# Where the first down product of a pair of chunks stands on TensorE

## The chip, the core and the metric

The kernel runs on one core of a Trainium2 chip. Its time is the device time of one execution in microseconds. Three runs of the kernel before the change took 606.92, 608.14 and 609.78 us; the median, 608.14 us, is the time before.

## What is computed

The input is `x` with 2048 tokens of 512 channels, in float32. Two branches read it and a gate mixes them:

```python
g = _sigmoid((x * gate_w).sum(-1, keepdims=True))
a = _A_ref(x, A_wqkv, A_wo)     # attention, 32 heads of 16, over 8 positions 2 apart
b = (_gelu(x @ w_gate) * (x @ w_up)) @ w_down      # 512 -> 1792 -> 512
return g * a + (1 - g) * b
```

The second branch, the FFN, is where the change lies. Its hidden layer has 1792 columns, which the kernel cuts into 14 chunks of 128.

## The kernel before

**Tokens.** The 2048 tokens are worked on in two halves of 1024, called `par` 0 and `par` 1. A half has two blocks `b` of four tiles `t` of 128 tokens. `ffn(0)` is the first FFN and `ffn(1)` the second; between them stand the projections of the second half's queries, keys and values (line 189). The attention itself runs on VectorE beside all of this.

**Precision.** A float32 operand is split into a high and a low part, and a product is three matmuls of 128x128 by 128x512: high times high, high times low, low times high. For a chunk's down weights the high part is made by ScalarE (line 484). The low part is a negated copy by ScalarE (line 481), to which a transfer issued by POOL adds the raw weights (line 482, `d<-r`). The gate and up weights `g` are made in the same way (lines 452, 453 and 457); two such transfers, of 384 and 512 KB, belong to a chunk, and one of 256 KB to its down weights.

**One chunk.** `gate_up` does the gate and up products of a chunk in seven block products of a 2x2 scheme, each of six matmuls (line 495): `a11`, `s1`, `s2`, `a12`, `s4`, `s3` and `a22`. The last of them, `a22`, is put off: `late` holds it and `fourth()` emits it in the next chunk, between that chunk's `s1` and `s2`. Between the products ScalarE applies the activation, VectorE adds and multiplies, and `hidden` leaves the chunk's hidden values as a high part `hh` (line 511) and a low part `hl` (line 512), one pair for each block `b`.

**The down product.** Chunks are taken in pairs; `gr` numbers the pairs from 0 to 6. While chunk `f` is done, `down(par, f // 2 - 1, t, b)` multiplies the pair before it with its down weights: chunk 6, for instance, begins the downs of pair 2, which are chunks 4 and 5. One call is six matmuls (line 538), three for each chunk of the pair (`i` is 0 or 1): `hh` with the high weights, `hh` with the low ones, `hl` with the high ones. For `b` 0 they add into one of four PSUM banks, `acc0` to `acc3`, which stay open through all seven pairs; for `b` 1 they go to a bank `p`, which ScalarE fills from `rt` and empties to it (lines 532 and 554). The first call of a pair, with `b` and `t` 0, is emitted in an even chunk right behind that chunk's `a11` product. The seventh pair's calls stand behind the loop over the chunks, after the last `fourth()`.

**What sets the order.** The order on each engine isn't that of the program text. A scheduler (the tile framework, with a model of the engines' times) takes the emitted instructions and may put a matmul ahead of others that were emitted before it, as soon as it holds its operands for ready. `ordered(ins, other)` forbids that for one pair of instructions: `ins` must then stand behind `other` on their engine. It adds no semaphore. `paced(ins)` adds one: the instruction then waits until the last emitted matmul is done. `LAST` holds the last matmul that was emitted. Work of the attention is pulled in by `pull` at a low priority.

In `down`, lines 538 to 542 are the ones of interest. `LAST` is set after every matmul, so a call for which the condition holds is chained as a whole: its first matmul stands behind the last one emitted before it, and its six follow in the order of the text. The condition takes `gr` 1, with `b` and `t` 0, in the first FFN. The other transfers that the prediction speaks of are `keep_parts` (line 470, `ws<-g`) and the loads of raw weights (lines 423 to 428).

Of the kernel before, what the change touches and what calls it, by code (L numbers as in the profile page):

```python
# [47 lines left out]
def tile_gated_mix(ctx: ExitStack, tc: tile.TileContext, xt, wqkv, wff, wo, out):  # L48
# [11 lines left out]
    def tl(tag, dt=F32):  # L60
        return pool.tile([P, COLS.get(tag, 512)], dt, name=tag, bufs=BUFS[tag])
# [5 lines left out]
    def bank(tag):  # L67
        return psum.tile([P, 512], F32, name=tag, bufs=BUFS.get(tag, 1))
# [291 lines left out]
    def ordered(ins, other):  # L360
        after(ins, other, mybir.DependencyClass.NoSync)
# [39 lines left out]
    def pull(budget, key=None):  # L401
        credit[0] += budget
        while credit[0] > 0 and (key is None or key not in done):
            with tc.high_priority(offset=-BEHIND):
                c = next(fill, None)
            if c is None:
                credit[0] = 0.0
                return
            credit[0] -= c
        if key:  # L410
            credit[0] = 0.0
# [105 lines left out]
    def pace(par, f):  # L517
        return PACE[2 if par else f > 5]
# [8 lines left out]
    def down(par, gr, t, b):  # L527
        if b == t == gr == 0:
            ACC.update((t, bank(f"acc{t}")) for t in range(BT))
        pp = bank("p") if b else ACC[t]  # L530
        if b and gr:
            nc.scalar.activation(pp, RT[BT + t], AF.Copy)  # L532
        ts = slice(t * P, (t + 1) * P)
        for i in range(2):
            hh_, hl_ = Hs[2 * gr + i, b]
            d = WD[2 * gr + i]
            for n, (a, w) in enumerate(((hh_, d[:, :512]), (hh_, d[:, 512:1024]), (hl_, d[:, :512]))):
                ins = nc.tensor.matmul(pp, a[:, ts], w, start=(i == 0 and n == 0 and gr == 0),  # L538
                                       stop=(i == 1 and n == 2), skip_group_check=True)
                if gr == 1 and b == t == 0 and not par:  # L540
                    ordered(ins, LAST[-1])
                LAST[:] = [ins]
        jj = BT * b + t
        if gr == NG - 1 and par:
            nc.scalar.activation(pp, pp, AF.Copy, scale=gc[:, par, jj:jj + 1])
            ACC[jj] = pp
        elif gr == NG - 1:
            st = tl("s")
            nc.scalar.activation(st, pp, AF.Copy, scale=gc[:, par, jj:jj + 1])
            nc.gpsimd.dma_start(out_v[2 * jj], st)  # L550
        elif b:
            if gr == 0:
                RT[BT + t] = tl("rt")
            nc.scalar.activation(RT[BT + t], pp, AF.Copy)  # L554
        pull(1.2 * pace(par, 2 * gr + 2))
# [87 lines left out]
    def ffn(par):  # L643
# [3 lines left out]
        for f in range(FC):  # L647
# [5 lines left out]
            if f > 1:  # L653
                pieces = [[lambda b=b, i=i: down(par, f // 2 - 1, f % 2 * 2 + i, b)] for b in range(2) for i in range(2)]
            else:
                tile_ = (lambda jj: project_one(1, jj)) if par else values
                pieces = [[lambda jj=jj: tile_(jj) for jj in jjs]
                          for jjs in (((0, 1), (2, 3), (4, 5), ()),
                                      ((6,), (7,), (), ()) if par else ((6, 7), (), (), ()))[f]]
# [48 lines left out]
        for b in range(2):  # L708
            for t in range(BT):
                down(par, NG - 1, t, b)  # L710
                if par and t == 0:
                    oT[0, b] = channels(par, 0, b)
                if not par and not b:
                    split_kq() if t % 2 else again(0, 1 + t)
                elif not par and b:
                    again(1, (2, 3, 0, 1)[t])
# [454 lines left out]
```

## Time and profile before

| | us |
|---|---|
| median of three runs | 608.14 |
| lowest and highest run | 606.92, 609.78 |
| the profiled execution, its own time | 609.76 |
| its span, from the first to the last instruction | 608.0 |
| TensorE busy with matmuls | 598.2 |
| VectorE busy | 526.5 |
| ScalarE busy | 382.9 |
| POOL busy | 79.1 |

The profiled execution took 609.76 us, and its span is 608.0 us of them. In a timeline row stand the start, the time, the engine, the line, the operation with its tiles, and how many instructions were merged; the bracket behind it tells the engine's idle time before and who ended it. Matmuls are pipelined: one of 512 columns is shown with 0.39 us, but the next starts 0.227 us after it.

### The profile page before, as it was taken

How to read it: one execution, taken by the hardware profiler on the slowest of the kernel's cores; microseconds unless marked ns; L12 is line 12 of the kernel's file. 1: busy time of each engine (PE TensorE's matmuls, PEld its weight loads, DVE VectorE, ACT ScalarE, POOL GpSimd, SP SyncE). 2: the span in 40 equal slices, each digit the busy share in tenths (PEclk: the TensorE clock that was granted, in tenths of full speed). 3: DMA queues.
4: the chain of work that ended last, by engine and by line, in shares of the span. 5: the costliest groups of instructions: out<-in, count | busy, mean ns of one | idle time of the engine just before them, and what ended most of it. 6: DMA issues, size and time to landing. Idle time of an engine off the chain costs nothing.

```text
span 608.0 us, 8192 instructions
## 1 busy us (share of the span) xinstructions
PE 598.2 (98%) x2802; PEld 498.2 (82%) x2802; DVE 526.5 (87%) x611; ACT 382.9 (63%) x650; POOL 79.1 (13%) x106
## 2 busy tenths in 40 slices
PE   9999999999999999989999999999999999999997
PEld 6889977788888887877899888888888888888885
DVE  5997969999898998798989988789899999999941
ACT  5845557777679776857364356566866676677531
POOL 0501001111111111102000001111101111101200
PEclk9999999999999999999999999999999999999999
DMA  7289896989889888976789979686888768937823
GB/s 279 85 252 246 241 275 172 271 237 271 206 248 260 223 255 230 253 205 181 253 218 335 252 221 271 146 256 158 228 207 213 207 182 217 259 88 207 125 50 138
DMA packets 84741, 131.03 MB, mean 216 GB/s; under 512 B 8030, under 2 KB 52317, under 8 KB 84700
## 3 DMA queue, kind: packets, MB, share of 16 engines
q1 hardware_dynamic: 63310, 94.01, 47.7%
q0 software_dynamic: 12096, 31.40, 27.3%
q10 hardware_dynamic: 9294, 5.11, 2.8%
q8 instruction: 22, 0.36, 0.2%
q14 instruction: 19, 0.16, 0.1%
HBM read 67.18 MB, written 36.77 MB: 171 GB/s over the span
## 4 chain that ended last, share of the span: by engine, by line
PE 71%; DMA 12%; issue 8%; DVE 4%; ACT 3%; SPq 1%; ACTq 0%; POOL 0%; POOLq 0%; DVEq 0%
PE p L495 29%; PE p L538 9%; PE acc L189 9%; PE acc L538 9%; PE p L767 5%; DMA d<-r 4%; DMA g<-raw 3%; PE p L834 3%; PE acc L834 3%; DMA ws<-g 3%; DVE prod L290 2%; PE p L189 2%; PE acc L767 2%; DMA kq<-qs 1%; DMA vs<-hl 1%
## 5 line engine op out<-in xcount | busy, mean ns | idle before, releaser
L495 PE MATMUL p<-S,g 128*128 128x512 f32 x672 | 166.5, 390 | 0.0
L495 PEld LDWEIGHTS p<-S,g 128*128 128x128 f32 x672 | 125.7, 188 | 26.5 <-ACT rt L554 0.5
L495 PE MATMUL p<-A,g 128*128 128x512 f32 x504 | 127.6, 390 | 0.1
L495 PEld LDWEIGHTS p<-A,g 128*128 128x128 f32 x504 | 94.3, 188 | 20.4 <-DMA g<-raw 0.6
L290 DVE TENSOR_TENSOR prod<-kq 128x2048 f32<-128x2048 f32 x32 | 73.0, 2281 | 12.3 <-DMA kq<-qs 4.6
L453 POOL DMA_DIRECT2D g<-raw x40 | 34.8, 870 | 319.0 <-ACT g L452 180.5
L331 DVE TENSOR_TENSOR prod<-v,lg 128x2048 f32<-128x2048 f32 x32 | 72.9, 2277 | 1.8 <-PE acc L538 1.3
L293 DVE TENSOR_REDUCE lg<-prod 128x128 f32<-128x2048 f32 x32 | 73.0, 2282 | 0.3
L538 PE MATMUL p<-d,hh 128*128 128x512 f32 x224 | 68.0, 390 | 1.0 <-ACT p L532 0.5
L538 PE MATMUL acc<-d,hh 128*128 128x512 f32 x224 | 61.3, 392 | 3.3 <-DMA d<-r 2.9
L538 PEld LDWEIGHTS acc<-d,hh 128*128 128x128 f32 x224 | 41.8, 188 | 13.5 <-DMA d<-r 3.8
L538 PEld LDWEIGHTS p<-d,hh 128*128 128x128 f32 x224 | 41.9, 188 | 10.5 <-ACT p L532 0.9
L457 ACT ACTIVATE g<-raw 128x1024 fp32r<-128x1024 f32 (+1 forms) x40 | 39.5, 990 | 13.3 <-PE p L495 13.3
L509 DVE TENSOR_TENSOR c<-c 128x512 f32<-128x512 f32 x56 | 38.2, 683 | 9.2 <-ACT c L606 8.8
L505 DVE TENSOR_TENSOR c<-p,s 128x512 f32<-128x512 f32 x56 | 37.9, 682 | 8.1 <-PE p L495 8.1
L500 ACT ACTIVATE s<-p 128x512 f32<-128x512 f32 x56 | 33.2, 592 | 18.1 <-PE p L495 16.5
L452 ACT ACTIVATE g<-raw 128x1024 fp32r<-128x1024 f32 (+1 forms) x40 | 39.5, 986 | 7.9 <-DVE raw L434 6.9
L538 PE MATMUL p<-d,hl 128*128 128x512 f32 x112 | 42.3, 390 | 0.0
L512 DVE TENSOR_TENSOR hl<-c,hh 128x512 fp32r<-128x512 f32 x56 | 38.3, 685 | 4.5 <-ACT hh L511 4.2
L511 ACT ACTIVATE hh<-c 128x512 fp32r<-128x512 f32 x56 | 35.1, 626 | 7.4 <-DVE c L509 6.5
L554 ACT ACTIVATE rt<-p 128x512 f32<-128x512 f32 x48 | 28.1, 592 | 18.1 <-PE p L538 17.8
L335 DVE TENSOR_TENSOR prod<-prod 128x1024 f32<-128x1024 f32 x32 | 39.0, 1219 | 0.3
(193 smaller groups left out, 916.2 us busy)
## 6 DMA issues: line engine op xcount, KB each, us to landing
g<-raw POOLq DMA_DIRECT2D x27, 512.0 KB, 6.1
raw<-wff SPq DMA_DIRECT2D x42, 256.0 KB, 3.4
ws<-g SPq DMA_DIRECT2D x14, 768.0 KB, 5.6
g<-ws SPq DMA_DIRECT2D x14, 768.0 KB, 5.1
r<-wff SPq DMA_DIRECT2D x28, 256.0 KB, 3.7
d<-r POOLq DMA_DIRECT2D x26, 256.0 KB, 7.2
g<-raw POOLq DMA_DIRECT2D x13, 384.0 KB, 7.5
v<-vs SPq DMA_DIRECT2D x8, 512.0 KB, 7.3
```

The costliest lines, as they stand in the source:

```text
L189: LAST[:] = [nc.tensor.matmul(ps[:, :cn], a[:, t], w[:, c0:c0 + cn], start=(kc == 0 and n == 0), stop=(kc == KC - 1 and n == 2))]
L290: paced(nc.vector.tensor_tensor(prod, spans(k, jj), q[:, jj:jj + 2, None, :].to_broadcast([P, 2, W, UC]), op=OP.mult))
L293: nc.vector.tensor_reduce(two_of(lg, jj), prod.rearrange("p j w (h d) -> p (j w) h d", d=DH), axis=AX.X, op=OP.add)
L331: paced(nc.vector.tensor_tensor(prod.rearrange("p j w (h d) -> p (j w) h d", d=DH), spans(v, jj).rearrange("p j w (h d) -> p j w h d", d=D ...
L335: nc.vector.tensor_tensor(prod[:, :, :4], prod[:, :, :4], prod[:, :, 4:], op=OP.add)
L452: nc.scalar.activation(lo, raw, AF.Copy, scale=-1.0)
L457: ins = nc.scalar.activation(hi, raw, AF.Copy)
L495: LAST[:] = [nc.tensor.matmul(ps, w_, a_, start=(start and kc == 0 and n == 0), stop=(kc == 1 and n == 2), skip_group_check=True)]
L509: nc.vector.tensor_tensor(ge, ge, up, op=OP.mult)
L512: nc.vector.tensor_tensor(hl_, ge, hh_.bitcast(F32), op=OP.subtract)
L538: ins = nc.tensor.matmul(pp, a[:, ts], w, start=(i == 0 and n == 0 and gr == 0), stop=(i == 1 and n == 2), skip_group_check=True)
L767: ins = nc.tensor.matmul(pa, a, b, start=(first and n == 0), stop=(last and n == 2), skip_group_check=True)
```

## The change

The condition for the chain loses its bound to the second pair. It then holds for `gr` 1 to 6 in the first FFN, so for five more calls: those of pairs 2 to 5, behind `a11` of chunks 6, 8, 10 and 12, and that of pair 6, behind `a22` of chunk 13. The second FFN (`par` 1) isn't touched.

```diff
             for n, (a, w) in enumerate(((hh_, d[:, :512]), (hh_, d[:, 512:1024]), (hl_, d[:, :512]))):
                 ins = nc.tensor.matmul(pp, a[:, ts], w, start=(i == 0 and n == 0 and gr == 0),
                                        stop=(i == 1 and n == 2), skip_group_check=True)
-                if gr == 1 and b == t == 0 and not par:
+                if gr and b == t == 0 and not par:
                     ordered(ins, LAST[-1])
                 LAST[:] = [ins]
```

## Prediction, made before the changed kernel was run

> **What bounds the kernel now.** I read the page's busy times first, then the stretches of the span, then what TensorE (PE) waited for.
>
> ```profile
> PE 598.2 (98%) x2802; PEld 498.2 (82%) x2802; DVE 526.5 (87%) x611; ACT 382.9 (63%) x650; POOL 79.1 (13%) x106
> 45.00:105.00 60.00, 59.20 (x350) 51.92 (x349) 51.60 (x52) 36.37 (x72) 5.78 (x7) 1.00 0.83 236
> 105.00:285.00 180.00, 176.40 (x771) 143.85 (x770) 163.11 (x200) 133.35 (x211) 28.67 (x35) 1.00 0.87 236
> 285.00:370.00 85.00, 85.00 (x466) 74.35 (x465) 76.91 (x90) 41.62 (x81) 7.10 (x10) 1.00 0.85 253
> 370.00:550.00 180.00, 180.00 (x796) 149.14 (x795) 163.86 (x172) 117.30 (x191) 20.93 (x25) 1.00 0.76 203
> ```
>
> The rows of stretches give length, then busy time of PE, its weight loads, DVE, ACT and POOL, the granted clock, the DMA share and GB/s. PE is busy for 98% of the span. From 285 to 550 us it has no idle time at all. In the first FFN's part that the change reaches (105 to 285) it is idle for 180.00 - 176.40 = 3.60 us. So PE's queue bounds the kernel, and the change, which removes no matmul, can win little more than those 3.6 us. What ended them:
>
> ```profile
> PE acc L538 <- DMA d<-r: 2.9, 2, 1.7
> PE p L538 <- ACT p L532: 0.5, 1, 0.5
> 228.28 0.39 PE L538 MATMUL acc<-d,hh 128*128 128x512 f32 x1
> 229.93 1.89 PE L538 MATMUL acc<-d,hh 128*128 128x512 f32 x7 [1.26 <-DMA d<-r]
> 257.05 1.52 PE L495 MATMUL p<-A,g 128*128 128x512 f32 x6
> 258.41 0.40 PE L538 MATMUL acc<-d,hh 128*128 128x512 f32 x1
> 260.49 1.89 PE L538 MATMUL acc<-d,hh 128*128 128x512 f32 x7 [1.68 <-DMA d<-r]
> 262.22 1.52 PE L495 MATMUL p<-A,g 128*128 128x512 f32 x6
> 275.35 0.73 PE L538 MATMUL p<-d,hh 128*128 128x512 f32 x2 [0.50 <-ACT p L532]
> ```
>
> Six matmuls take 258.41 - 257.05 = 1.36 us, so one takes 0.227. Twice the second matmul of a pair's first down product, `hh` times the low weights, comes late, because POOL's transfer `d<-r` of chunk 10 (229.9) and chunk 12 (260.5) hasn't landed. Against the 0.227 us in which it would have followed, the stalls are 229.93 - 228.28 - 0.23 = 1.42 and 260.49 - 258.41 - 0.23 = 1.85 us.
>
> **The change part by part.** Nothing is added or removed: the changed program has the same 2802 matmuls, and `ordered` brings no wait. Its order on PE shows what moves. In pairs 2, 3, 4, 5 and 6 the first chunk's three matmuls into `acc0` leave the odd chunk, where the scheduler had put them ahead, and stand behind `a11` of the next even chunk (behind `a22` of chunk 13 for pair 6). That is 5 x 3 x 0.227 = 3.4 us of PE work, each piece of 0.68 us some 13 us later. What stood between comes up to 0.68 us earlier, and in a few places more. Whether this costs anything depends on how long operands had been ready. An example, `s1` of chunk 5:
>
> ```profile
> 138.33 1.08 ACT L554 ACTIVATE rt<-p 128x512 f32<-128x512 f32 x2
> 138.09 1.98 PE L538 MATMUL acc<-d,hh 128*128 128x512 f32 x8
> 140.81 2.88 PE L495 MATMUL p<-S,g 128*128 128x512 f32 x12
> ```
>
> Its bank was freed by the first of the two ACT copies, at about 138.9, and it started at 140.81: 1.9 us of cover against a shift of 0.68. I cost the moved pieces themselves at nothing, for that cover; with the cover gone they cost 0.68 us a pair. The scheduler also reshuffled neighbours, and there I find six terms.
>
> (a) Chunk 12's `d<-r`. Before, POOL issued it third:
>
> ```profile
> 245.28 0.86 POOL L453 DMA_DIRECT2D g<-raw  x1 [9.78 <-ACT g L452]
> 248.12 0.86 POOL L453 DMA_DIRECT2D g<-raw  x1 [1.98 <-ACT g L452]
> 249.64 0.86 POOL L482 DMA_DIRECT2D d<-r  x1 [0.66 <-ACT d L481]
> 249.64 10.80 DMA d<-r
> ```
>
> Now it stands ahead of the 512 KB `g<-raw` and its ACT copy comes 1.5 us earlier, behind an `s1` that itself starts 1.8 us earlier. Besides, PE asks later: the six `a22` matmuls of chunk 12 now stand ahead of the first `acc` matmul, so the low weights are wanted at 258.64 + 1.36 = 260.0. Landing was 249.64 + 10.80 = 260.44; 1.5 us earlier it is 258.9. The 1.85 us stall goes: -1.9 us (bounds -1.9, and -1.4 if nothing but the six matmuls counts).
>
> (b) Chunk 7's `g`, for `a11`:
>
> ```profile
> 157.83 0.86 POOL L482 DMA_DIRECT2D d<-r  x1 [12.24 <-ACT d L481]
> 158.57 1.01 POOL L453 DMA_DIRECT2D g<-raw  x1
> 158.57 7.42 DMA g<-raw
> 165.29 3.31 PE L495 MATMUL p<-A,g 128*128 128x512 f32 x12
> 180.68 2.88 PE L495 MATMUL p<-A,g 128*128 128x512 f32 x12
> ```
>
> The twelve matmuls at 165.29 take 0.43 us more than the same twelve at 180.68: `g` landed at 165.99, in their midst. Now it is issued ahead of `d<-r`, which comes 0.74 us behind or later and has slack. -0.4 us (0 to -0.4).
>
> (c) Chunk 8's `d<-r` goes the other way, behind the 512 KB `g<-raw` of chunk 9:
>
> ```profile
> 187.70 0.86 POOL L453 DMA_DIRECT2D g<-raw  x1 [11.83 <-ACT g L452]
> 189.22 0.86 POOL L482 DMA_DIRECT2D d<-r  x1 [0.66 <-ACT d L481]
> 190.17 0.86 POOL L453 DMA_DIRECT2D g<-raw  x1
> g<-raw POOLq DMA_DIRECT2D x1, 512.0 KB, 9.1
> d<-r POOLq DMA_DIRECT2D x1, 256.0 KB, 7.5
> 198.36 1.98 PE L538 MATMUL acc<-d,hh 128*128 128x512 f32 x8
> ```
>
> It landed at 189.22 + 7.5 = 196.7, the other at 190.17 + 9.1 = 199.3: the queue lands in the order of issue, 2.5 us for the 512 KB. In the new order `d` is last and lands at about 199.3, and PE wants the low weights at 198.36 + 0.23 = 198.6. A new stall of +0.7 us; 0 if the transfer isn't held up, 1.7 if it is also issued 1 us later.
>
> By the Trainium skill (DMA: Bandwidth & Descriptors, "Anatomy of one DMA — SWDGE (gpsimd) path") a transfer issued by GpSimd takes an estimated 2.0 us plus its bytes at 436 GB/s, 2.6 us for these 256 KB, and there would be no new stall: the sum below would be 0.7 us lower. The trace has 7.5 us for this one.
>
> (d) Pair 2's whole product now stands as one block ahead of `a22` of chunk 5, so chunk 5's low weights are wanted 1.36 us sooner:
>
> ```profile
> 143.78 0.86 POOL L482 DMA_DIRECT2D d<-r  x1 [0.94 <-ACT d L481]
> DMA to landing us min/median/max: 8.1/8.1/8.1
> 153.05 1.98 PE L538 MATMUL acc<-d,hh 128*128 128x512 f32 x8
> ```
>
> They landed at 151.9 and were wanted at 153.28, now at 151.9. Between 0 and 0.7 us, near the row's 0, since the ACT copy ahead of the issue follows an `s1` that is itself 0.68 us earlier: +0.2. `a22` behind the block is 1.8 us later, and its `hl` had about that much slack: +0.1 (0 to 0.5).
>
> (e) Chunk 13's first `g`. Two DVE subtractions stood ahead of ACT's copy; now the second stands behind the attention's product:
>
> ```profile
> 242.29 1.15 DVE L434 TENSOR_TENSOR raw<-raw 128x512 f32<-128x512 f32 x2
> 244.11 2.29 DVE L290 TENSOR_TENSOR prod<-kq 128x2048 f32<-128x2048 f32 x1
> 244.14 0.84 ACT L452 ACTIVATE g<-raw 128x768 fp32r<-128x768 f32 x1
> DMA to landing us min/median/max: 10.2/10.2/10.2
> ```
>
> The subtraction ends at about 245.6 instead of 243.4, ACT's copy starts 1.5 us later, and the transfer that landed at 245.28 + 10.2 = 255.5 lands at up to 257.0. PE's third matmul of `a11` wants it at 257.50. 0 to 1.0 us, for a transfer that is 1 us slower than that; +0.3.
>
> (f) Chunk 10's `d<-r` (229.9) keeps its place on POOL, while PE's work ahead of its ACT copy comes up to 0.9 us earlier: 0 to -0.9, I take -0.3. The 0.5 us at 275.35 stay: that bank is freed by two ACT copies that follow a PE product 0.68 us ahead, whenever that comes.
>
> Sum: -1.9 - 0.4 + 0.7 + 0.2 + 0.1 + 0.3 - 0.3 = -1.3 us. Behind 285 us the orders of the other engines differ by single neighbours, and no matmul there loses its cover. Against the profiled execution's own 609.76 us this gives 608.5, its span 606.7. That execution lies 1.6 us above the median and within the runs shown, so I take the difference from the median: 608.14 - 1.3 = 606.8 us.
>
> **The rivals.** *The hole stays open.* The three matmuls were cover for the products of the odd chunk; taken away, each pair meets a wait 0.68 us sooner and pays its 0.68 us again later. This is the one mechanism that makes it slower: 5 x 0.68 = 3.4 us, with no stall removed, gives 611.5. It decides from the point where operands are ready less than 0.68 us ahead. For it speaks that DVE is busy for 163 of the 180 us, and DMA engines for 0.87 of the time. Against it: the 1.9 us at `s1` of chunk 5, and only 3.6 us of idle time to show that PE runs into anything. Chance 0.15.
>
> By the Trainium skill (TensorE: Matmul & The Clock Gate, "What's actually happening") an idle window of about 3.4 us halves TensorE's clock. The longest stall here is 1.68 us at a granted clock of 1.00, so no run here shows it.
>
> *All late weights come in time.* If (f) frees the whole 1.42 us, the 0.5 at 275 goes, and (c), (d) and (e) cost nothing, the sum is -1.9 - 0.4 - 1.4 - 0.5 = -4.2, 603.9. Against it: the queue's order at chunk 10 is the old one. Chance 0.10.
>
> *Transfers don't hold each other up.* Without (c) it is -2.0, 606.1; the landings 2.5 us apart speak against it. Chance 0.10, within the forecast's class.
>
> *Nothing moves in time:* what (a) wins, (c) and (e) take back at their upper bounds: -1.9 - 0.4 + 1.7 + 0.2 + 0.1 + 1.0 - 0.3 = +0.4, 608.5. Chance 0.15, same class.
>
> **How the numbers follow.** The forecast itself has 0.50. What a measurement can tell from no change is about 0.5%, 3.0 us. Faster by more: 0.10; slower by more: 0.15; within: 0.50 + 0.10 + 0.15 = 0.75. The terms' bounds add to -3.2 and +2.5 us, so 604.9 to 610.6; the slower case pulls the upper end to 611.0 and the faster one the lower to 604.3.
>
> **What would show it.** PE's wait for `d<-r` at about 260 is gone, that at 230 stays with 0.5 to 1.4 us, a new one of up to 1 us stands at about 198, and none at `a11` of chunk 7. From 285 us on PE has no idle time. Wrong would be: idle time of PE at `s1`, `s4` or `s3` of the odd chunks (the hole), at `a11` of chunk 13 (e too small), or anywhere in the second FFN.

## The result, and the profile after

The changed kernel took 605.83 us (median of 10 runs, 604.67 to 607.09) against 607.97 us for the kernel before (10 runs, 606.37 to 610.23): a ratio of 0.9959, with a 95% interval of 0.9941 to 0.9977. A second series, run with the experiments, gave 606.06 against 607.33 us, 0.9980 (0.9967 to 0.9992). The kernel is 1.3 to 2.1 us faster, and below the 0.5% that the prediction called the bound of what can be told from no change. The predicted time was 606.8 us, 1.3 us less than before.

The profiled execution of the changed kernel took 605.68 us, 603.9 of them its span. First its busy times, from the page, then the stretches that the prediction showed of before (length, then busy time of PE, its weight loads, DVE, ACT and POOL, granted clock, DMA share, GB/s):

```profile
PE 597.0 (99%) x2802; PEld 497.9 (82%) x2802; DVE 525.1 (87%) x611; ACT 383.4 (63%) x650; POOL 79.0 (13%) x106
```

```profile
105.00:285.00 180.00, 179.45 (x788) 147.09 (x788) 166.18 (x207) 134.93 (x213) 29.99 (x38) 1.00 0.88 239
285.00:370.00 85.00, 85.00 (x466) 74.31 (x465) 77.27 (x87) 42.79 (x83) 5.42 (x7) 1.00 0.88 260
370.00:550.00 180.00, 180.00 (x796) 149.04 (x795) 162.01 (x172) 117.82 (x188) 20.94 (x25) 1.00 0.76 204
```

From 105 to 285 us PE was idle for 3.60 us before and is idle for 180.00 - 179.45 = 0.55 us now; from 285 to 550 us it has no idle time, as before. What PE waited for (us in total, times, longest):

```profile
PE p L78 <- DVE zero L72: 1.1, 1, 1.1
PE p L538 <- ACT hh L511: 0.5, 1, 0.5
PE p L538 <- ACT p L532: 0.5, 1, 0.5
PE acc L538 <- DVE d L87: 0.5, 1, 0.5
PE acc L834 <- ACT g L834: 0.3, 1, 0.3
```

The 2.9 us for `d<-r` are gone from the list. The timeline shows the three places in question: the first products that want the low weights of chunks 8, 10 and 12.

```profile
197.65 1.52 PE L538 MATMUL acc<-d,hh 128*128 128x512 f32 x6
...
227.57 1.69 PE L538 MATMUL acc<-d,hh 128*128 128x512 f32 x6
...
257.68 1.52 PE L538 MATMUL acc<-d,hh 128*128 128x512 f32 x6
```

At each place the matmul with the low weights, the second of the six, stands in the same row as the first; before, it began a row of its own with a bracket at 229.93 and 260.49. The POOL issues behind them:

```profile
188.78 0.86 POOL L482 DMA_DIRECT2D d<-r  x1
...
217.89 0.86 POOL L482 DMA_DIRECT2D d<-r  x1
...
245.21 0.86 POOL L453 DMA_DIRECT2D g<-raw  x1 [12.22 <-ACT g L452]
246.21 0.86 POOL L482 DMA_DIRECT2D d<-r  x1
250.48 0.86 POOL L453 DMA_DIRECT2D g<-raw  x1 [3.40 <-ACT g L452]
```

Chunk 12's `d<-r` stands ahead of the 512 KB transfer, as the prediction read from the order.

**How much of this is one execution's luck.** The two profiled executions differ by 608.0 - 603.9 = 4.1 us, the medians by 2.1 and 1.3. I added, over all matmuls of a trace, the time from one start to the next beyond what the matmul's columns take (0.227 us for 512), where it was over 0.05 us. This gives 10.4 us for the profiled execution of before and 6.3 for the changed kernel; taken from the spans, 597.6 us are left in both. So the whole difference is stalls of PE. But the profiled execution of before, 609.76 us, was long for its kernel: of the ten runs beside the changed kernel three were longer, and their median is 607.97. The first experiments therefore ran both kernels again for a second profile.

### The profile page after: what moved, and what is told of

The parts are those of the page before. It is cut to its first block, busy times and chain, and to the rows that moved or that the text cites. A ratio compares the mean times of both kernels' runs of the same rounds, so it can differ in the third digit from the quotient of the medians.

```text
span 603.9 us, 8190 instructions
## 1 busy us (share of the span) xinstructions
PE 597.0 (99%) x2802; PEld 497.9 (82%) x2802; DVE 525.1 (87%) x611; ACT 383.4 (63%) x650; POOL 79.0 (13%) x106
## 4 chain that ended last, share of the span: by engine, by line
PE 87%; DMA 5%; DVE 3%; ACT 3%; issue 1%; SPq 1%; DVEq 0%; ACTq 0%
PE p L495 40%; PE p L538 12%; PE acc L538 12%; PE acc L189 9%; PE p L767 5%; PE p L834 3%; PE acc L834 3%; PE p L189 2%; PE acc L767 2%; DMA kq<-qs 1%; DMA raw<-wff 1%; DVE prod L290 1%; DMA ws<-g 1%; DMA raw<-xt 1%; DMA ks<-hl 0%
## 5 line engine op out<-in xcount | busy, mean ns | idle before, releaser
L538 PEld LDWEIGHTS p<-d,hh 128*128 128x128 f32 x224 | 41.8, 188 | 10.5 <-ACT hh L511 0.9
```

## The experiments

All kernels compute the whole of the reference. Theory T: the gain is PE's waits for POOL's late transfers. Theory R: the gain comes from where the matmuls stand on PE.

**Both kernels once more.** No edit.

> The kernel before, unchanged, for a second profile of it. If the stalls at 230 and 260 are a property of its order, both are there again with 0.5 us or more; if they are the mark of a late execution (the first profiled one took 609.8 us, 2.4 us above the median), only their sum over an execution of median length is there, about 1.5 us in one or two places. Ratio 1.000.

> The changed kernel, unchanged, for a second profile and a ratio on the same chip as the others. No wait for d<-r of over 0.5 us; ratio 0.996 to 0.9975.

The kernel before measured 606.74 us against 607.33 for itself, 0.9991 (0.9978 to 1.0005); so about 0.1% is what such a comparison leaves open. The changed kernel gave the 0.9980 named above, a smaller gain than the 0.996 to 0.9975 expected. Timeline of PE in the second profile of before:

```profile
226.61 0.39 PE L538 MATMUL acc<-d,hh 128*128 128x512 f32 x1
227.92 1.89 PE L538 MATMUL acc<-d,hh 128*128 128x512 f32 x7 [0.92 <-DMA d<-r]
...
256.40 0.39 PE L538 MATMUL acc<-d,hh 128*128 128x512 f32 x1
257.21 1.89 PE L538 MATMUL acc<-d,hh 128*128 128x512 f32 x7 [0.42 <-DMA d<-r]
```

POOL's issues of these two transfers, same profile:

```profile
217.34 0.86 POOL L482 DMA_DIRECT2D d<-r  x1 [0.23 <-ACT d L481]
...
247.63 0.86 POOL L482 DMA_DIRECT2D d<-r  x1 [0.66 <-ACT d L481]
```

Both stalls are there again, but as 227.92 - 226.61 - 0.23 = 1.08 and 257.21 - 256.40 - 0.23 = 0.58 us: 1.7 us together where the first profile had 3.3. The late `g` at 166 isn't there. In the second profile of the changed kernel two short waits appear:

```profile
196.96 0.39 PE L538 MATMUL acc<-d,hh 128*128 128x512 f32 x1
197.52 1.43 PE L538 MATMUL acc<-d,hh 128*128 128x512 f32 x5 [0.17 <-DMA d<-r]
...
227.34 0.39 PE L538 MATMUL acc<-d,hh 128*128 128x512 f32 x1
228.02 1.43 PE L538 MATMUL acc<-d,hh 128*128 128x512 f32 x5 [0.29 <-DMA d<-r]
```

They are 0.33 us at chunk 8 and 0.45 us at chunk 10. With this the waits can be laid out as a room and a duration. The room is the time from POOL's issue to the moment at which PE asks (the start of the first product plus 0.227 us). For chunk 12 before it was 258.41 + 0.23 - 249.64 = 9.00 us in the first profile and 256.40 + 0.23 - 247.63 = 9.00 in the second.

| low weights of | kernel | room, us | time to landing in the profiles, us |
|---|---|---|---|
| chunk 12 | before | 9.00, 9.00 | 10.8, 9.5 |
| chunk 12 | changed | 11.70, 11.70 | 6.6, 6.1 |
| chunk 10 | before | 9.51, 9.50 | 10.9, 10.5 |
| chunk 10 | changed | 9.91, 9.90 | 9.9, 10.3 |
| chunk 8 | before | 9.36, 9.36 | 7.5, 5.8 |
| chunk 8 | changed | 9.10, 9.10 | 8.7, 9.4 |

The room belongs to the kernel's order: two executions agree within 0.01 us. The time to landing differs between two executions of one kernel, here by up to 1.7 us. Where it is longer than the room, PE stalls for the difference.

**POOL's order against PE's order.** The change moves three pairs of transfers on POOL, besides the matmuls. Two kernels take them apart: `poolonly` is the kernel before with only these three swaps, `undoabc` the changed kernel with only these three put back. Behind every transfer its instruction is noted, and `ordered` holds the pairs:

```diff
+    TR, PUT = {}, ((12, (0, 13, 1)), ((0, 7, 0), 6), ((0, 9, 1), 8))
+    put = lambda k, ins: TR.setdefault(k, ins) is ins and [ordered(TR[x], TR[y]) for x, y in PUT if k in (x, y) and x in TR and y in TR]
...
-        nc.gpsimd.dma_start(lo.bitcast(F32), raw, accum_op=OP.add)
+        put((par, f, i), nc.gpsimd.dma_start(lo.bitcast(F32), raw, accum_op=OP.add))
...
-        nc.gpsimd.dma_start(d[:, 512:1024].bitcast(F32), rd, accum_op=OP.add)
+        put(f, nc.gpsimd.dma_start(d[:, 512:1024].bitcast(F32), rd, accum_op=OP.add))
```

This is `undoabc`; in a pair the first stands behind the second, a bare number is that chunk's `d<-r`, and (0, 13, 1) is chunk 13's second `g` in the first FFN. `poolonly` has each pair the other way round.

> The kernel before with POOL's transfers in the order of the changed kernel: chunk 12's d<-r ahead of chunk 13's second g, chunk 7's first g ahead of chunk 6's d<-r, chunk 9's second g ahead of chunk 8's d<-r. The orders on PE, DVE, ScalarE and the queue of the loads are those of before. Theory T (the gain is in the order of POOL's transfers): ratio 0.996, as the changed kernel. Theory R (the gain is in PE's order): ratio 1.000, and a new wait for d<-r near 198 in the profile.

> The changed kernel with POOL's transfers put back into the order of before; the orders on PE, DVE, ScalarE and the queue of the loads are those of the changed kernel. Theory T: ratio 1.000, with the wait for chunk 12's d<-r at 260 back (about 1 us, as it now lands 2.5 us later than in the changed kernel and had 5 us of margin at most). Theory R: ratio 0.9965, no wait for d<-r over 0.3 us, as PE asks for chunk 12's low weights 1.36 us later than before.

`poolonly` measured 606.12 against 607.33 us, 0.9978 (0.9966 to 0.9991): all of the changed kernel's 0.9980 on the same chip, without a matmul moved. `undoabc` measured 607.97 us, 1.0019 (0.9999 to 1.0038): nothing is left of the gain. The ratio that R gave lies outside both intervals; only its new wait near 198 came. The gain is near what the comparison can show: beside the twelve runs of `again_before` alone (606.74), the changed kernel and `poolonly` are 0.7 and 0.6 us faster, which twelve runs each don't clearly tell from nothing; the 1.9 us between `undoabc` and either of them do stand out. PE's waits for the weights in `poolonly`, then its product at 258:

```profile
PE acc L538 <- DMA d<-r: 0.9, 2, 0.6
```

```profile
257.82 1.98 PE L538 MATMUL acc<-d,hh 128*128 128x512 f32 x8
```

The waits are at 198 (0.52 us) and at 229 (0.73); at 258 eight matmuls run through, so the one at 260 is gone. In `undoabc` it is back, by PE's timeline:

```profile
258.57 0.39 PE L538 MATMUL acc<-d,hh 128*128 128x512 f32 x1
259.85 1.43 PE L538 MATMUL acc<-d,hh 128*128 128x512 f32 x5 [0.89 <-DMA d<-r]
```

The stall is 259.85 - 258.57 - 0.23 = 1.05 us, although PE asks behind the six `a22` matmuls. My figure for R, that this later demand alone would do, was wrong for a reason in ScalarE's order: the changed kernel makes chunk 13's second `g` late there (POOL issues it at 250.48 behind 3.40 us of waiting), so a `d<-r` behind it is issued at 251.91 and has 6.9 us of room, less than before. `undoabc` thus exaggerates the loss, and how much of it is this can't be told from it. `poolonly` is the fairer of the two tests: it shows that POOL's order is enough for the gain. What PE's order alone would win, no run shows.

**One swap, two swaps.** `df13` and its repetition `again_a` are the kernel before with the first of the three swaps alone, `bc` has the other two.

```diff
+    DL = []
+    behind = lambda ins, when: ordered(ins, DL[-1]) if when and DL else None
...
-        nc.gpsimd.dma_start(lo.bitcast(F32), raw, accum_op=OP.add)
+        behind(nc.gpsimd.dma_start(lo.bitcast(F32), raw, accum_op=OP.add), i and f == 13 and not par)
...
-        nc.gpsimd.dma_start(d[:, 512:1024].bitcast(F32), rd, accum_op=OP.add)
+        DL[:] = [nc.gpsimd.dma_start(d[:, 512:1024].bitcast(F32), rd, accum_op=OP.add)]
```

For `bc` the pairs of `poolonly` without chunk 12:

```diff
-    TR, PUT = {}, (((0, 13, 1), 12), (6, (0, 7, 0)), (8, (0, 9, 1)))
+    TR, PUT = {}, ((6, (0, 7, 0)), (8, (0, 9, 1)))
```

> The kernel before, with one thing changed: on POOL chunk 12's d<-r (256 KB) stands ahead of chunk 13's second g<-raw (512 KB) instead of behind it. The orders on PE, DVE, ScalarE and the queue of the loads are those of before, so no matmul moves. Theory T (PE waits for low weights that POOL's queue lands late): the transfer lands about 2.5 us sooner, the stall of 1.85 us at 260 goes, the one at 230 (1.42 us) and the late g at 166 (0.43 us) stay; ratio 0.997, 1.9 us less. Theory R (what the change wins comes from where the three matmuls of a pair stand on PE, the landing is a side show): the idle time moves to the next wait, ratio 1.000.

> Once more the kernel before with chunk 12's d<-r alone ahead of chunk 13's second g on POOL; its first ratio was 1.0001, with five of twelve executions at a mean clock of 0.998 or less. Theory T1 (each stall is worth what it lasts, so this swap saves the wait at 260, which was 0.58 and 1.85 us in two profiles of the kernel before): ratio 0.9975 to 0.999, and the first result was a batch with many late landings at 230. Theory T2 (the wait saved at 260 comes back elsewhere, so this swap is worth nothing and the other two carry the gain): ratio 1.000 again and a wait in this profile that neither profile of before has.

> The kernel before with the other two of the three swaps on POOL: chunk 7's first g ahead of chunk 6's d<-r, chunk 9's second g ahead of chunk 8's d<-r. No other engine's order changes. T1: the late g at 166 (0 to 0.4 us) goes, a wait of 0.3 to 0.5 us comes at 198, the stalls at 230 and 260 stay; ratio 0.9995 to 1.0005. T2: ratio 0.998, as with all three swaps, and the wait at 260 is gone although its transfer keeps its place.

`df13` gave 1.0001 (0.9985 to 1.0018), `again_a` 0.9990 (0.9979 to 1.0002), `bc` 0.9993 (0.9982 to 1.0005). None can be told from the kernel before alone; by these ratios the swap of chunk 12 is worth 0 to 0.6 us, the other two 0.4, and the three together 1.3. That fits T1 (parts that add up) within these intervals and doesn't prove it. Where a profile shows the swap of chunk 12, it does its work. POOL's row in `again_a`, then the time to landing of that transfer, then PE's row:

```profile
248.37 0.86 POOL L482 DMA_DIRECT2D d<-r  x1 [3.50 <-ACT d L481]
```

```profile
DMA to landing us min/median/max: 5.4/5.4/5.4
```

```profile
257.14 2.01 PE L538 MATMUL acc<-d,hh 128*128 128x512 f32 x8
```

The room is again 257.14 + 0.23 - 248.37 = 9.00 us; without the 512 KB ahead of it the 256 KB land in 5.4 us instead of 9.5 to 10.8, and eight matmuls run through. All the profiles say the same of this wait: it is there in the four of kernels without the swap (1.85, 0.58, 1.05 and 0.24 us) and in none of the ten with it. In `bc`, where the transfer keeps its place, it took 9.2 us and PE waited 0.24: T2, by which the other two swaps would free it, falls. The profiled execution of `df13`, with 609.23 us the second longest of its twelve, has a loss of its own, which belongs to the stall at 230:

```profile
227.09 0.39 PE L538 MATMUL acc<-d,hh 128*128 128x512 f32 x1
229.74 2.40 PE L538 MATMUL acc<-d,hh 128*128 128x512 f32 x7 [2.27 <-DMA d<-r]
231.94 4.02 PE L495 MATMUL p<-S,g 128*128 128x512 f32 x12
235.79 0.39 PE L495 MATMUL p<-A,g 128*128 128x512 f32 x1
```

The stretches of that place, the granted clock third from the end:

```profile
230.00:231.00 1.00, 1.00 (x5) 0.80 (x5) 1.00 (x1) 0.62 (x2) 0.61 (x1) 0.95 1.11 210
231.00:232.00 1.00, 1.00 (x4) 0.72 (x3) 1.00 (x2) 0.00 (x0) 0.25 (x1) 0.50 0.95 239
232.00:233.00 1.00, 1.00 (x4) 0.81 (x3) 0.40 (x1) 0.00 (x0) 0.00 (x0) 0.50 1.05 298
233.00:234.00 1.00, 1.00 (x3) 0.78 (x3) 0.00 (x0) 0.00 (x0) 0.00 (x0) 0.50 1.10 275
234.00:235.00 1.00, 1.00 (x5) 0.80 (x4) 0.00 (x0) 0.38 (x1) 0.00 (x0) 0.84 1.06 240
```

Here chunk 10's low weights took 11.9 us for a room of 9.50. PE was idle for 2.27 us, and then the clock was granted at half from about 231 to 234.3: twelve matmuls took 235.79 - 231.94 = 3.85 us instead of 2.72, and the seven ahead of them 2.20 instead of 1.59, 1.7 us lost in all. This stall was paid once while waiting and again behind it. The swap doesn't touch that transfer. Three of the twelve executions of `df13` were at 608 us or more with a mean clock of 0.998 or less (four in all had such a clock, not the five that the expectation of `again_a` names); none of `again_a` was. They don't explain the null result: the median of the other nine is 606.92 us, 0.4 below the kernel before. Why that series had more of them stays open.

**More swaps, on both kernels.** `dfall` and `dfall_after` put `d<-r` of every chunk, not only of the even ones that the expectations below name, ahead of the next chunk's second `g`, on the kernel before and on the changed one:

```diff
-        behind(nc.gpsimd.dma_start(lo.bitcast(F32), raw, accum_op=OP.add), i and f == 13 and not par)
+        behind(nc.gpsimd.dma_start(lo.bitcast(F32), raw, accum_op=OP.add), i and not par)
```

> The kernel before, with d<-r of every even chunk of the first FFN put ahead of the next chunk's second g<-raw on POOL; this swaps two transfers at chunks 3, 10, 11 and 12 and nothing on the other engines. Theory T: both long stalls go, at 230 (1.42 us) and 260 (1.85 us), the late g at 166 stays; 3.3 us less, ratio 0.9946, or 0.996 if the landings are early enough only in part of the executions. Theory R: no matmul moves, ratio 1.000. If the g that now lands later is wanted at once, a new wait at a11 or s1 of chunk 11 or 13 of up to 2 us, ratio 0.999 to 1.000.

> The changed kernel, with d<-r of every even chunk put ahead of the next chunk's second g<-raw on POOL as well. Theory T: the changed kernel shows no wait for d<-r, with margins of 0.05 us at chunk 10 and 0.4 us at chunk 8; these grow, so the median stays at that of the changed kernel or gains up to 0.5 us (ratio 0.995 to 0.996) and the spread of its executions shrinks. Theory R: as the changed kernel, 0.996. If the later g is wanted at once: 0.997 to 0.999.

`dfall` gave 1.0010 (0.9996 to 1.0023), which misses T's 0.9946 to 0.996; `dfall_after` gave 0.9982 (0.9967 to 0.9997), the case of a later `g` that is wanted at once. PE in `dfall`:

```profile
125.57 2.11 PE L495 MATMUL p<-A,g 128*128 128x512 f32 x8 [1.08 <-DMA g<-raw]
...
228.89 1.98 PE L538 MATMUL acc<-d,hh 128*128 128x512 f32 x8
...
258.39 2.12 PE L538 MATMUL acc<-d,hh 128*128 128x512 f32 x8 [0.77 <-ACT hh L511]
```

The stalls for `d<-r` at 230 and 260 are gone, as T said, and two others have taken their place: chunk 4's `g` is late at 125.6, since it now stands behind a `d<-r` (in `dfall_after` 1.59 us of idle time at the same place), and at 258 PE waits for ScalarE's `hh`. I had expected a late `g` only at chunks 11 and 13.

The last two kernels leave chunk 3 alone. `before_plus` is the kernel before with swaps of chunks 6, 10 and 12; `a_after_plus` is the changed kernel with chunk 8's `d<-r` put back ahead and chunk 10's put ahead.

```diff
-    TR, PUT = {}, (((0, 13, 1), 12), (6, (0, 7, 0)), (8, (0, 9, 1)))
+    TR, PUT = {}, (((0, 13, 1), 12), (6, (0, 7, 0)), ((0, 11, 1), 10))
```

```diff
-    TR, PUT = {}, ((12, (0, 13, 1)), ((0, 7, 0), 6), ((0, 9, 1), 8))
+    TR, PUT = {}, (((0, 9, 1), 8), ((0, 11, 1), 10))
```

> The kernel before, its orders on PE, DVE, ScalarE and the queue of the loads kept, with three swaps on POOL: chunk 7's first g ahead of chunk 6's d<-r, chunk 10's d<-r ahead of chunk 11's second g, chunk 12's d<-r ahead of chunk 13's second g. T1: no wait for d<-r or for g of more than 0.3 us, ratio 0.9965 to 0.9975 and so at least as fast as the changed kernel. T2: not below 0.9985, as the waits come back at another transfer.

> The changed kernel with two more swaps on POOL: chunk 8's d<-r back ahead of chunk 9's second g (its wait at 198 was 0 and 0.33 us in two profiles), and chunk 10's d<-r ahead of chunk 11's second g (its wait at 228 was 0 and 0.45 us). The other engines' orders are those of the changed kernel. T1: no wait for d<-r; 0.4 us below the changed kernel, ratio to the kernel before 0.997 where the changed kernel has 0.998 on this chip. T2 (the swap of chunk 8 is part of the gain): ratio 0.9985 to 1.000.

`before_plus` measured 607.31 against 607.21 us, 1.0002 (0.9988 to 1.0015); T1 had 0.9965 to 0.9975 and fails here. Its profile has no wait for `d<-r`, but two rows, of ScalarE and of PE, show a new one:

```profile
251.17 0.63 ACT L484 ACTIVATE d<-r 128x512 fp32r<-128x512 f32 x1 [1.34 <-DMA r<-wff]
...
255.60 0.62 ACT L511 ACTIVATE hh<-c 128x512 fp32r<-128x512 f32 x1
```

```profile
256.27 2.11 PE L538 MATMUL acc<-d,hh 128*128 128x512 f32 x8 [1.05 <-ACT hh L511]
```

ScalarE waits 1.34 us for the load of chunk 13's raw down weights (line 484); `hh` (line 511) stands behind that on ScalarE, and PE waits for it. Two things bring this about. Beside `again_before`, ScalarE ends the work ahead of the wait 1.4 us earlier, with the stall at 230 gone; and the load lands 3 us later, at 251.07 instead of 248.10. The same two waits are in `dfall` (1.07 and 0.77 us). They don't account for the median of `before_plus`: the execution that shows them took 605.79 us, 1.5 us less than that median. Why the median is that of the kernel before stays open. In the changed kernel's order `hh` stands ahead of that copy on ScalarE:

```profile
254.47 0.62 ACT L511 ACTIVATE hh<-c 128x512 fp32r<-128x512 f32 x1
254.99 0.62 ACT L484 ACTIVATE d<-r 128x512 fp32r<-128x512 f32 x1
```

Besides, PE has six `a22` matmuls more ahead of the product. There the same POOL swap meets no such wait: `a_after_plus` measured 605.46 against 607.21 us, 0.9975 (0.9964 to 0.9986), the lowest median of all. Its interval overlaps that of the changed kernel, so it beats the kernel before but isn't shown to beat the changed one. All that PE waited for a transfer there:

```profile
PE p L495 <- DMA g<-raw: 0.2, 1, 0.2
```

**What else sets a landing.** Chunk 12's `d<-r` has the same place on POOL in the changed kernel and in `a_after_plus`, yet it took 6.6 and 6.1 us in the profiles of the one and 10.8 in that of the other, where PE asked after 12.2 us and so didn't wait. What differs near it is the start of the loads on SyncE's queue (`SPq`). Its rows in the first profile of the changed kernel, then in `a_after_plus`, with the time to landing of that `d<-r`:

```profile
239.83 1.32 SPq L107 DMA_DIRECT2D raw<-xt  x2
...
241.90 0.38 SPq L470 DMA_DIRECT2D ws<-g  x1
```

```profile
243.22 1.33 SPq L107 DMA_DIRECT2D raw<-xt  x2
...
245.29 0.38 SPq L470 DMA_DIRECT2D ws<-g  x1
```

```profile
DMA to landing us min/median/max: 10.8/10.8/10.8
```

These loads of about 2 MB start 5.4 us ahead of POOL's first transfer for chunk 13 in the one and 1.9 us in the other. The swap of chunk 10 is probably behind it: chunk 11's second `g`, which now stands behind a `d<-r`, lands at 229.45 instead of 226.22, and the next load of SyncE, which waits for that `g`, is issued at 229.57 instead of 226.34. In all four kernels with chunk 10's swap the loads start 0.4 to 3.0 us ahead, and chunk 12's `d<-r` takes 7.9 to 10.8 us; in the six others in which it stands ahead of the 512 KB, 4.1 to 6.6 us ahead, and it takes 5.4 to 6.6. So the place on POOL alone doesn't set the landing. That the start of the loads does isn't shown, since no run changes them by themselves.

**One hold alone.** `h15` keeps, of the five added holds, that of pair 5.

```diff
-                if gr and b == t == 0 and not par:
+                if gr in (1, 5) and b == t == 0 and not par:
```

> The condition holds for the pairs 1 and 5 alone, so of the five added holds one is kept: the three matmuls of pair 5 stand behind a11 of chunk 12. On POOL only chunk 12's d<-r moves, ahead of the 512 KB g<-raw. Theory T: the stall at 260 goes, those at 230 and 166 stay, 1.9 us less, ratio 0.997. Theory R: one fifth of the changed kernel's gain of 2.1 us, 0.4 us less, ratio 0.9993. The hole (each moved piece costs its 0.68 us): 0.7 us more, ratio 1.001.

It measured 606.09 against 607.32 us, 0.9976 (0.9962 to 0.9990), near T's 0.997. In its profile the wait at 260 is gone, and those at 230 (1.23 us) and for `g` at 166 (0.46 us) are there. Yet the same swap on POOL without the hold was worth less: `df13`, on the same chip, is 1.1 us slower, `again_a`, on another, 0.4 us. The intervals of `h15` and of both overlap, so it stays open whether the hold adds to the swap.

## Why the prediction was right

The time was right, and so was the mechanism: PE's queue bounds the kernel, the change moves matmuls whose operands are long ready, and what it wins is waits for low weights. The runs show that POOL's order is enough for that; what PE's order would win alone they don't show. Term by term:

- **(a), -1.9.** The wait at 260 is gone in both profiles of the changed kernel. The term was sized on one late execution; the second profile of before has 0.58 us there, and the swap alone measured 0 to 0.6 us. The room grew by 2.7 us, near the 1.5 + 1.36 that I had from the earlier issue and the later demand. That the landing itself gets shorter by 3 to 4 us in these profiles I had left out, and it would have done alone: in `poolonly` and `again_a` the room stays at 9.00 us, the landing is 6.2 and 5.4, and the wait is gone. The later demand would have done too: in `a_after_plus` a landing of 10.8 us cost nothing.
- **(b), -0.4.** No wait at `a11` of chunk 7 in either profile; but the second profile of before had none either. 0 to 0.4.
- **(c), +0.7.** The sign is right and the price too high: 0 and 0.33 us, and 0.52 in `poolonly`. The landing rose from 7.5 and 5.8 us to 8.7 and 9.4. By the figure of the Trainium skill (DMA: Bandwidth & Descriptors, "Anatomy of one DMA — SWDGE (gpsimd) path"), an estimated 2.6 us, there would be no new stall; that fits one of the two profiles, and the 2.6 us fit neither.
- **(d) and (e), +0.6 together.** No such wait in either profile of the changed kernel. In the first, chunk 13's first `g` landed at 251.50 and was wanted at 255.41. (e) isn't impossible: in `a_after_plus` it landed at 255.6, and 0.34 us were lost.
- **(f), -0.3.** This is the term that failed in size. I wrote that the wait at 230 "stays with 0.5 to 1.4 us"; it was 0 and 0.45, where two profiles of before had 1.42 and 1.08. ScalarE's copy came earlier, as I said: the room rose by 0.40 us. The landing was 0.2 to 1.0 us shorter as well, and I had no term for that.
- **The 0.5 us at 275 stay.** They do, at 270.6, as the list of waits shows (`p` from line 532). From 285 to 550 us PE still has no idle time.
- **The moved pieces at nothing.** The hole would have cost 3.4 us, a ratio of 1.0056. The kernel that has the holds without POOL's new order, `undoabc`, measured 1.0019 with an upper end of 1.0038, and from 110 to 285 us its profile has three stalls of 0.15 us or more: two for `d<-r` and the one at `p` from line 532. None is at `s1`, `s4` or `s3`. This rival falls.
- **Transfers don't hold each other up.** Falls too: chunk 8's `d<-r` took 5.5 to 7.5 us in the ten profiles in which it stands ahead of the 512 KB, and 8.0 to 9.4 in the four in which it stands behind them.
- **All late weights come in time.** But for the 0.5 us at 275, this is what the first profile of the changed kernel shows. Yet the 603.9 us that I gave for it weren't reached: I took the whole 4.2 us off the median, and the stalls they consist of were those of an execution 1.6 us above it. The forecast mixes the two in the same way.

The sum of -1.3 came out near the measured -2.1 and -1.3 us partly by luck, because errors of both signs met: (a) was too large for a median execution, the costs (c) to (e) were too large as well, and (f) too small. What the prediction lacked was a second look at the same kernel. Its terms took durations of transfers from one execution to a hundredth of a microsecond, while two executions of one kernel differ by up to 1.7 us in just these durations, and the same transfer at the same place on POOL differs by 4 us between the changed kernel and `a_after_plus`.

## What to carry to other kernels

Split every wait for a transfer into the room that the order gives it (from issue to demand, here the same to 0.01 us in two executions) and the time to landing (here different by up to 1.7 us), and ask of a change which of the two it moves; a margin smaller than that spread can be a wait in another execution. A change that reorders matmuls can owe its whole gain to a few transfers that change places on another queue: do those swaps alone before believing in the matmuls. And a swap that removes a wait can bring others: in `dfall` a late `g` and, behind a late load, a late `hh` cost PE 1.9 us of idle time together, and its time was that of the kernel before.

## What the runs showed of the hardware

After a wait of 2.27 us on PE, in one execution of `df13`, the granted clock went from 1.00 to 0.50 for some 3.4 us, which cost 1.7 us more than the wait itself. It fell at about 230.9, 1.2 us after PE had begun again. Waits of up to 1.68 us left the clock at 1.00. The Trainium skill (TensorE: Matmul & The Clock Gate, "What's actually happening") puts the fall behind an idle window of about 3.4 us; here an idle time of two thirds of that came before the fall. Its length of the slow phase, one busy window of the same 3.4 us, agrees with the trace.

The eleven `d<-r` between 105 and 262 us, all of 256 KB, in the second profile of the kernel before:

```profile
DMA to landing us min/median/max: 4.4/7.8/13.7
```

One size thus lands after 4.4 to 13.7 us in one execution. Its place behind a larger transfer (chunk 8: 8.0 to 9.4 us against 5.5 to 7.5) and the start of the loads on SyncE's queue (chunk 12: 10.8 against 6.6) go with a part of that.
